# A fused attention and expert kernel on one core: rows for the experts gathered one block ahead instead of two, and the last attention pair's fills and value products in another order

## Chip, cores, metric

One Trainium2 chip, one of its cores. The metric is device time of one execution in microseconds (us), the median of several runs; smaller is better.

## What is computed

Attention with rotary embedding over 8 batches, 8 heads, 576 tokens, head width 64, and then a top-1 mixture of 8 experts on the 4608 resulting rows of 512 numbers:

```python
scores = q_rot @ k_rot.T / sqrt(D);  attn = softmax(scores);  x = attn @ v     # all heads side by side
logits = x @ w_gate + modality_bias[modality_id]                               # 4608 x 8
e_idx = argmax(logits);  gate_w = softmax(logits)[e_idx]
for e in range(E):
    mask = e_idx == e
    h = np.maximum(x[mask] @ w1[e], 0.0)                                       # 512 -> 1024
    out[mask] = gate_w[mask, None] * (h @ w2[e])                               # 1024 -> 512
```

Which token goes to which expert is known only on the chip.

## The kernel before

**Attention.** 32 pairs of heads, one about every 14.4 us. Each pair `n` has nine score tiles (`scores`, `rowmin`, `expo`), six *fills* (`fill`: the probabilities are transposed on TensorE into a ring of three two-bank PSUM tiles), two *evacuations* of each fill to SBUF (`evac`, one on ScalarE, one on VectorE), two value products (`AV`, half 0 = "AVA" for 256 columns, half 1 = "AVB" for 320), their copies (`avout`, "OTA" and "OTB"), the output transposes (`outp`) and the scaling (`ev`, "EVA" and "EVB"). The value products and the output transposes share the PSUM pool `psA` with two buffers, tag `pa`.

AVB reads the columns that fills F2, F3 and FB fill; AVA reads those of F0, F1 and FA.

**Routing.** After every fourth pair (a batch) the router ranks the rows of its batch by expert, and GpSimd scatters their numbers into a table in DRAM (`scatter`, five indirect DMAs a batch, "TAB" in the profile).

**Experts.** The table is read in blocks of 256 rows. 8 blocks are planned after five batches (they run first), 11 more after all eight: 19 blocks on this input. For each block `s`, eight indirect DMAs of GpSimd (`m_gather`, "XG<-X" at line 734) fetch 128 quarter rows each into `XG[s % 2]`; before the first of them a small GpSimd instruction makes the list of indices (`iy`, line 732). VectorE transposes both halves (`m_tr`, gathers 0 to 3 make the first half, 4 to 7 the second), ScalarE and VectorE split them into a high and a low part (`m_tre`); `m_split` does the same for the weights (`W1H` and `W2H` by ScalarE, `W1L` and `W2L` by VectorE). The first layer is four groups of 24 matmuls (`m_l1`, line 799; tiles psH, or ps for block 0), the second two groups of 24 (`m_l2`, line 816). The results are scaled by ScalarE into `y` (two buffers, line 819) and scattered to the output by GpSimd (line 820, "out_dram"). Each such scatter writes the same tensor as the one before it.

Engines keep the order of the program. In the attention part that order is sorted by due times written by hand (`KEYS` for a pair, with other values for single pairs in `AT`: `last` is the last pair, number 31); in the expert part it is the order of the loop in `chain`. With 31*14.438 us subtracted, an entry of `AT` is a due time in the frame of the last pair. Everything due after `end` = 12.0 is written behind the attention part; block 0's first layer (keys `l1`) is still in it.

In `chain`, block `s` begins with `m_rows(s + 2)`: all eight gathers of the block behind the next one. They wait for nothing but the list and for `m_tre(s)` having read the buffer. Block 1's eight gathers stand in the attention part (`rows[1]`, behind the first group of block 0's first layer) and those of block 2 at key 16.5, behind the first two scatters of batch 6 and ahead of its last three. Batch 7's five scatters come out of the list `late`, popped by `one()`: two at the end of block 1, three within the first layer of block 2.

Of the kernel before, what the change touches and what calls it, by code (L numbers as in the profile page):

```python
# [45 lines left out]
AT = dict(  # L46
    rk=(23.0, 28.55, 31.2, 36.9, 41.45, 43.0, 44.4, 45.7, 54.6, 56.9, 57.4, 58.85, 60.2, 70.35, 73.3),
    bias=15.6,
    sc=(73.4, 87.85, 102.3, 116.7, 116.75),
    sce=(73.4, 73.45, 87.85, 87.9, 102.3),  # L50
    pl=(58.9, 70.4, 73.35, 84.85, 87.75, 99.3, 102.2, 113.7, 116.6),
    plan=(-49.7, -35.2, 6.0, 9.0),
    ix=(-41.5, -3.9, 6.1, 9.1),
    sine=-48.9,
    rows=(((0, -27.5, None), (1, -13.05, None), (2, -12.4, None), (3, -2.9, (30, "av", 0)), (5, 0.45, (30, "av", 1)),
           (7, 4.75, (30, "out", 1))), ((0, 11.15, ("l1", 0)),), ((0, 16.5, None),)),
    w1=(-21.6, -21.5, -16.2, -16.1),
    w2=(-9.9, -9.8, -9.7, -9.6),
    hi=(-14.8, -14.7, -0.4, -0.3),
# [2 lines left out]
    te=(10.3, 10.4),  # L62
    hi2=(10.5, 10.98, 11.1, 11.2),
    lo2=(11.5, 11.55, 11.65, 11.75),
    last=dict(AVA=10.3, AVB=10.4, RE=10.2, RI=10.25, OTA=10.96, OTB=11.0, OUTB=11.2, OUTA=11.21, EVB=11.35, EVA=11.4, XO=11.9),
    l1=(11.1, 11.3, 11.4, 11.42),
    l1e=(11.3, 11.6, 11.7, 11.8),
    w1n=(11.85, 11.86, 11.87, 11.88),
# [2 lines left out]
    first=dict(S1=-5.9, S0=-5.86, MN1=-5.82, MN0=-5.74, EX1=-5.7, EX0=-5.66, S6=-5.58, S7=-5.54, MN6=-5.5,  # L71
        EX6=-5.42, MN7=-5.34, EX7=-5.3, S3=-5.26, S2=-5.22, MN3=-5.18, EX3=-5.14, F0=-5.1, MN2=-5.06,
        A_F0=-5.02, B_F0=-4.98, EX2=-4.94, F3=-4.9, S4=-4.86, A_F3=-4.82, B_F3=-4.78, MN4=-4.74, S5=-4.7,
        EX4=-4.66, MN5=-4.62, EX5=-4.58, S8=-4.54, MN8=-4.5, EX8=-4.46, LV=-2.9),
    second=dict(T1=-20.22, T2=-20.06, R=-19.9, HI=-19.82),
# [8 lines left out]
def tile_attention_moe(ctx: ExitStack, tc: tile.TileContext, qk, v, mod, wg, mb, w1, w2, rope, cf, ci, out):  # L84
# [23 lines left out]
    def cview(name):  # L108
        o, n = CF_OFF[name]
        return CF[:, o:o + n]  # L110
# [582 lines left out]
    def bank(kind):  # L693
        if kind in banks:
            return banks[kind].tile([P, 512], F32, name=f"ps{kind}", tag=f"ps{kind}")
        if not spare:
            ps = ring()[1]
            spare.extend(ps[:, i, :] for i in (1, 0))
        return spare.pop()
# [28 lines left out]
    def m_gather(s, t, g, after=None):  # L728
        d = ms[s]
        if "iy" not in d:  # L730
            d["iy"] = ixp.tile([P, 8], I32, name="iy", tag="iy")
            nc.gpsimd.tensor_scalar(d["iy"], d["xi"][:, :, 0], 4.0, cview("I4"), op0=ALU.mult, op1=ALU.add)
        rows = (N if slots[s][0] else NPL * S) * 4
        inst = nc.gpsimd.indirect_dma_start(out=XG[s % 2][:, t, g, :], out_offset=None,  # L734
                                            in_=X.rearrange("n (i f) -> (n i) f", f=P)[0:rows],
                                            in_offset=bass.IndirectOffsetOnAxis(ap=d["iy"][:, 2 * g + t:2 * g + t + 1], axis=0),
                                            bounds_check=rows - 1, oob_is_err=False)
        if after is not None:

            tc.add_manual_dep(inst.ins, (l1_[after[1]] if after[0] == "l1" else st[after[0]][after[1:]]).name,  # L740
                              mybir.DependencyInfo(mybir.DependencyClass.Sync, mybir.DependencyReason.DATA), reason="place")

    def m_rows(s):
        for t in range(2):
            for g in range(4):
                m_gather(s, t, g)

    def m_load1(s, g):
        d = ms[s]
        nc.sync.dma_start(out=ST1[:, :, g * 256:(g + 1) * 256],  # L750
                          in_=w1[bass.ds(d["e"], 1), :, g * 256:(g + 1) * 256].rearrange("o (c p) f -> p (o c) f", p=P), cond=d["c"])

    def m_load2(s, g):
        d = ms[s]
        nc.sync.dma_start(out=ST2[:, g * 2:g * 2 + 2, :],
                          in_=w2[bass.ds(d["e"], 1), g * 256:(g + 1) * 256, :].rearrange("o (c p) f -> p (o c) f", p=P), cond=d["c"])

    def m_hi(i, g):
        sl = slice(g * 256, (g + 1) * 256)
        if i == 0:  # L760
            acopy(W1[0][:, :, sl], ST1[:, :, sl])
        else:
            acopy(W2[0][:, g * 2:g * 2 + 2, :], ST2[:, g * 2:g * 2 + 2, :])

    def m_lo(i, g):
        sl = slice(g * 256, (g + 1) * 256)
        if i == 0:
            sub(W1[1][:, :, sl], ST1[:, :, sl], W1[0][:, :, sl].bitcast(F32))
        else:
            sl = slice(g * 2, g * 2 + 2)  # L770
            sub(W2[1][:, sl, :], ST2[:, sl, :], W2[0][:, sl, :].bitcast(F32))

    def m_split(i, g):
        m_hi(i, g)
        m_lo(i, g)
# [13 lines left out]
    def m_l1(s, g):  # L789
        d = ms[s]  # L790
        if g == 0:
            d["hh"], d["hl"] = HHL[s % 2]
        ps = bank("H").rearrange("p (c r) -> p c r", r=BLK)
        for i in range(2):
            f0 = (g * 2 + i) * P
            m = 0
            for c in range(4):
                for w, x in ((W1[0], XTH), (W1[0], XTL), (W1[1], XTH)):
                    l1_[s] = nc.tensor.matmul(ps[:, i, :], w[:, c, f0:f0 + P], x[:, c, :], start=(m == 0), stop=(m == 11)).ins  # L799
                    m += 1  # L800
        d["ps", g] = ps
# [24 lines left out]
    def J(k_, nm, n, f, *a):  # L826
        jobs.append((k_ + PER * n, len(jobs), f, a))
# [27 lines left out]
        load(2, half)  # L855
    z = NPAIR - 1

    OV = {0: AT["first"], 1: AT["second"], z: AT["last"]}
    for n in range(NPAIR):
        def K_(nm, f, *a):  # L860
            J(OV.get(n, {}).get(nm, K[nm]), nm, n, f, *a)

# [31 lines left out]
        if n % 4 == 3:  # L894
            K_("XO", xout, n // 4)
            g = route(n // 4)
            steps = [(next, g, None)] * (NRK - (n == z))
            scats = [(scatter, n // 4, j) for j in range(5)]
            if n == z:

                g = plan()
# [4 lines left out]
            if n == 4 * NPL - 1:  # L906
                g = plan0()
# [6 lines left out]
    def Z(k_, f, *a):  # L914
        J(k_, "moe", z, f, *a)

    A = AT
    fills = max(K[f] for f in K if f[0] in "SF")
    planned, tabled = (max(AT[c]) - (NPAIR - 4 * NPL) * PER for c in ("pl", "sc"))
    assert min(A["plan"]) > planned and min(A["ix"]) > tabled and min(A["w1"]) > max(K["T2"], K["LO"] - PER)  # L920
    assert min(A["w2"]) > max(K["T1"], K["LO"]) and min(A["te"]) > max(K[f"S{u}"] for u in range(9)) - PER
    assert min(A["hi2"]) > fills + 0.05 and min(A["lo2"]) > A["last"]["AVB"] + 0.05 and min(A["l1"]) > fills
    for s in range(len(A["plan"])):
        Z(A["plan"][s], m_plan, s)
    for s in range(4):
        Z(A["ix"][s], m_ix, s)
    for s in range(3):
        for i in range(8):
            k_, after = [x for x in A["rows"][s] if x[0] <= i][-1][1:]
            Z(k_ + 0.01 * i, m_gather, s, i // 4, i % 4, after)  # L930
# [27 lines left out]
    def prefetch(s):  # L958
        for i in range(3):
            m_plan(s + i)  # L960
        for g in range(4):
            m_load1(s, g)
        for i in range(3):
            m_ix(s + i)
        for i in range(2):
            m_rows(s + i)
        for g in range(4):
            m_load2(s, g)

    def chain(lo, hi, begun):  # L970
        if not begun:
            for g in range(4):
                m_split(0, g)
            for t in range(2):
                m_tr(lo, t)
                m_tre(lo, t)
        for s in range(lo, hi):
            nxt = s + 1 < hi
            if nxt:
                if s + 2 < hi and (not begun or s > 0):  # L980
                    m_rows(s + 2)
                if s + 3 < hi and (not begun or s > 0):
                    if s + 3 not in ms:
                        m_plan(s + 3)
                    m_ix(s + 3)
                for g in range(4):
                    if not begun or s > 0:
                        m_load1(s + 1, g)
            if not begun or s > lo:
                for g in range(4):  # L990
                    m_split(1, g)
                    m_l1(s, g)
                    m_l1e(s, g)
                    one()
            if nxt:
                for t in range(2):
                    m_tr(s + 1, t)
                for t in range(2):
                    m_tre(s + 1, t)
                    one()  # L1000
                for g in range(4):
                    m_load2(s + 1, g)
            if not begun or s > lo:
                m_l2(s, 0)
            if nxt:
                m_split(0, 0)
                one()
                m_split(0, 1)
                one()
            m_l2(s, 1)  # L1010
            if nxt:
                m_split(0, 2)
                one()
                m_split(0, 3)
                one()
# [108 lines left out]
```

## Time and profile before

| | |
|---|---|
| three runs | 937.27, 939.65, 940.5 us; median 939.65 |
| the profiled execution | 946.46 us, of which the span 944.7 us from first to last instruction |
| mean granted TensorE clock | 0.995 |
| TensorE matmuls (PE) | 903.4 us busy, 96% of the span, 9248 instructions |
| VectorE (DVE) | 670.6 us, 71% |
| ScalarE (ACT) | 629.9 us, 67% |
| GpSimd (POOL) | 669.0 us, 71%, 498 instructions |
| gathers, line 734 | 152, 1235 ns mean |
| scatters to the output, line 820 | 38, 1128 ns mean |

The attention part ends at about 500 us, the rest is the expert blocks. PE is busy almost everywhere, so the time is the sum of PE's work and of the gaps in it; the gaps lie between 486 and 561 us, in the passage from one part to the other. In rows of the profile "idle before <-X" names what ended an engine's idle time; "issue" is time in which it waited for nothing that the profile shows.

### The profile page before, as it was taken

What the parts mean: (1) busy time and instruction counts of PE and PEld (TensorE: products, weight loads), DVE (VectorE), ACT (ScalarE), POOL (GpSimd) and SP (SyncE); (2) the same over time, 40 slices, a digit from 0 to 9 for tenths busy, and PEclk for the clock granted to TensorE, in tenths of its full rate; (3) what the DMA queues carried; (4) which work ended last, traced back from release to release, by engine and by line L of the source; (5) the groups of instructions that cost most, each with busy time, mean ns of one, the idle gap of its engine ahead of it and who ended that gap; (6) DMA issues with size and microseconds to landing.
All of it is one profiled execution on the core that took longest, in us unless ns stands there. A gap on an engine that the chain in (4) does not pass through costs nothing. (4 is left out here: it accounts for less than half of the span.)

```text
span 944.7 us, 24944 instructions
## 1 busy us (share of the span) xinstructions
PE 903.4 (96%) x9248; PEld 740.9 (78%) x9248; DVE 670.6 (71%) x1165; ACT 629.9 (67%) x1292; POOL 669.0 (71%) x498
## 2 busy tenths in 40 slices
PE   2999999999999999999989999999999999999996
PEld 2777777777777777777667878888888899999995
DVE  6677778787787877877784768676666766666661
ACT  2778778787787877878881555565665656666561
POOL 3988879888888898999723768766676656666400
PEclk9999999999999999999999999999999999999998
DMA  8865758768586686855922621117711611251100
GB/s 261 237 185 166 236 159 213 188 167 229 162 222 165 183 213 175 232 163 154 244 98 73 186 72 35 46 57 229 230 51 51 229 40 45 90 190 45 37 24 16
DMA packets 79292, 136.90 MB, mean 145 GB/s; under 512 B 28699, under 2 KB 50603, under 8 KB 78140
## 3 DMA queue, kind: packets, MB, share of 16 engines
q1 hardware_dynamic: 68460, 114.06, 42.8%
q0 software_dynamic: 9440, 19.46, 6.3%
q10 hardware_dynamic: 1264, 1.72, 0.6%
q8 instruction: 75, 1.23, 0.6%
q14 instruction: 53, 0.43, 0.2%
HBM read 140.59 MB, written 19.77 MB: 170 GB/s over the span
## 5 line engine op out<-in xcount | busy, mean ns | idle before, releaser
L328 ACT ACTIVATE P<-ps,mn 128x576 f32<-128x576 f32 x288 | 210.4, 737 | 92.4 <-DVE mn L321 91.9
L321 DVE TENSOR_REDUCE mn<-ps 128x1 f32<-128x576 f32 x288 | 204.1, 745 | 93.5 <-PE ps L312 55.6
L734 POOL DMA_INDIRECT XG<-X,iy x152 | 187.7, 1235 | 70.9 <-issue 53.5
L799 PE MATMUL psH<-HL,W1H 128*128 128x256 f32 x1152 | 205.5, 281 | 1.0 <-issue 0.7
L312 PE MATMUL ps<-SW 64*128 64x288 f32 x960 | 166.5, 314 | 16.0 <-DMA SW<-HL 16.0
L799 PEld LDWEIGHTS psH<-HL,W1H 128*128 128x128 f32 x1152 | 177.9, 188 | 4.1 <-issue 2.5
L312 PE MATMUL ps<-HL 64*128 64x288 f32 x960 | 166.4, 312 | 1.0 <-ACT P L328 0.8
L799 PE MATMUL psH<-HL,W1L 128*128 128x256 f32 x576 | 161.7, 281 | 1.4 <-issue 0.8
L312 PEld LDWEIGHTS ps<-SW 64*128 64x128 f32 x960 | 134.2, 189 | 27.4 <-DMA SW<-HL 15.5
L312 PEld LDWEIGHTS ps<-HL 64*128 64x128 f32 x960 | 136.4, 189 | 22.7 <-issue 13.6
L269 DVE TENSOR_TENSOR W1L<-ST,W1H 128x1024 fp32r<-128x1024 f32 x76 | 90.1, 1222 | 80.6 <-ACT W1H L272 77.5
L390 PE MATMUL pa<-PH,V 128*64 128x320 f32 (+1 forms) x1024 | 138.3, 412 | 2.7 <-ACT oT L272 1.4
L820 POOL DMA_INDIRECT out_dram<-y,ix x38 | 42.9, 1128 | 129.7 <-ACT y L819 97.4
L816 PE MATMUL psY<-W2H,SW 128*128 128x512 f32 x304 | 121.2, 399 | 0.0
L816 PE MATMUL psY<-W2L,SW 128*128 128x512 f32 x304 | 119.9, 394 | 0.0
L334 PE MATMUL ps<-idf,P 64*128 64x64 f32 x2624 | 105.3, 229 | 8.5 <-ACT P L328 2.8
L334 PEld LDWEIGHTS ps<-idf,P 64*128 64x128 f32 x2624 | 92.2, 140 | 23.8 <-ACT PH L272 9.5
L799 PEld LDWEIGHTS psH<-HL,W1L 128*128 128x128 f32 x576 | 108.4, 188 | 1.8 <-issue 1.0
L289 POOL TENSOR_TENSOR HL<-ST,HL 128x1216 fp32r<-128x1216 f32 x31 | 86.1, 2777 | 31.8 <-ACT HL L272 31.7
L390 PEld LDWEIGHTS pa<-PH,V 128*64 128x64 f32 x1024 | 68.1, 136 | 51.1 <-issue 10.1
L366 DVE COPY PH<-ps 128x512 f32<-128x512 f32 (+1 forms) x160 | 96.0, 633 | 8.9 <-PE ps L334 7.6
L269 DVE TENSOR_TENSOR W2L<-ST,W2H 128x1024 fp32r<-128x1024 f32 x76 | 92.6, 1219 | 5.2 <-ACT W2H L272 4.3
(173 smaller groups left out, 1589.9 us busy)
## 6 DMA issues: line engine op xcount, KB each, us to landing
ST<-in_moe_w_dram SPq DMA_DIRECT2D x152, 512.0 KB
ST<-in_qk_dram SPq DMA_DIRECT2D x62, 608.0 KB
SW<-HL SPq DMA_DIRECT2D x124, 232.0 KB
V<-in_v_dram SPq DMA_DIRECT2D x32, 256.0 KB
X<-X SPq DMA_DIRECT2D x8, 1024.0 KB
XG<-X,iy POOLq DMA_INDIRECT x152
V<-in_v_dram SPq DMA_DIRECT2D x64, 16.0 KB
X<-XT SPq DMA_DIRECT2D x16, 64.0 KB
```

The lines of the kernel that those rows point to most:

```text
L269: nc.vector.tensor_tensor(o, a, b, op=ALU.subtract)
L289: e.tensor_tensor(d["HL"][:, 1, c], a, d["HL"][:, 0, c].bitcast(F32), op=ALU.subtract)
L312: free(nc.tensor.matmul(ps[:, g, 0:288], t[:, wq, q0:q0 + P], t[:, wk, k0:k0 + 288], start=(m == 0), stop=(m == len(L) - 1)), seen)
L321: lastmin[d["ring", u]] = nc.vector.tensor_reduce(mn, d["S", u][:, :, 0:288], op=ALU.min, axis=AX.XY).ins
L328: nc.scalar.activation(p.rearrange("p (a b) -> p a b", a=2), ps[:, :, 0:288], AF.Exp, bias=d.pop(("m", u)), scale=-1.0, accum_out=d["sum"] ...
L334: free(nc.tensor.transpose(ps[0][:, g, c:c + 64], src[r, k0:k0 + P], idf[r, r]), ps[1])
L366: mine.append((nc.vector.tensor_copy if g else acopy)(o, i).ins)
L390: i = nc.tensor.matmul(pa[hh * 64:hh * 64 + 64, 0:c1 - c0], d["V"][:, hh, kt, :], r, start=(kt == 0), stop=(kt == 4))
L734: inst = nc.gpsimd.indirect_dma_start(out=XG[s % 2][:, t, g, :], out_offset=None, in_=X.rearrange("n (i f) -> (n i) f", f=P)[0:rows], in_o ...
L799: l1_[s] = nc.tensor.matmul(ps[:, i, :], w[:, c, f0:f0 + P], x[:, c, :], start=(m == 0), stop=(m == 11)).ins
L816: nc.tensor.matmul(ps, hx[:, c, t * P:(t + 1) * P], w[:, c, :], start=(m == 0), stop=(m == 23))
L820: nc.gpsimd.indirect_dma_start(out=out, out_offset=bass.IndirectOffsetOnAxis(ap=d["ix"][:, t, 0:1], axis=0), in_=y, in_offset=None, bounds ...
```

## The change

Three edits.

1. **Gathers.** `m_rows` is gone. In `chain`, block `s` now gathers for block `s + 1`, two gathers ahead of each group of the first layer; from the second pair on, each waits for the last first-layer matmul written so far, that is for the group before. The gathers of block 1 in the attention part are spread the same way (one pair behind each of the four groups of block 0), and those of block 2 leave their place ahead of batch 6's last three scatters for the loop.
2. **Last pair.** Its fills go in the order F3, F0, F2, FB, FA, F1 (before: F3, F0, FA, F2, FB, F1), with their evacuations; AVB stands ahead of AVA, and their copies likewise.
3. **Last pair but one.** Its EVA moves from due time 25.51 to 24.55 (10.11 in the last pair's frame, just ahead of both value products; before it was due at 11.07, behind them).

```diff
-    rows=((...), ((0, 11.15, ("l1", 0)),), ((0, 16.5, None),)),
+    rows=((...), ((0, 11.15, ("l1", 0)), (2, 11.33, ("l1", 0)), (4, 11.365, ("l1", 0)), (6, 11.43, ("l1", 0)))),
...
-    last=dict(AVA=10.3, AVB=10.4, RE=10.2, RI=10.25, OTA=10.96, OTB=11.0, OUTB=11.2, OUTA=11.21, EVB=11.35, EVA=11.4, XO=11.9),
+    last=dict(F2=7.0, A_F2=7.75, B_F2=7.75, FB=7.5, A_FB=8.3, B_FB=8.3, FA=8.35, A_FA=8.8, B_FA=8.8, AVB=10.3, AVA=10.4, RE=10.2,
+              RI=10.25, OTB=10.96, OTA=11.0, OUTB=11.2, OUTA=11.21, EVB=11.35, EVA=11.4, XO=11.9),
+    last2=dict(EVA=24.55),
...
-    def m_rows(s):
-        for t in range(2):
-            for g in range(4):
-                m_gather(s, t, g)
...
-    OV = {0: AT["first"], 1: AT["second"], z: AT["last"]}
+    OV = {0: AT["first"], 1: AT["second"], z - 1: AT["last2"], z: AT["last"]}
...
-    for s in range(3):
+    for s in range(2):
         for i in range(8):
             k_, after = [x for x in A["rows"][s] if x[0] <= i][-1][1:]
             Z(k_ + 0.01 * i, m_gather, s, i // 4, i % 4, after)
...
-                if s + 2 < hi and (not begun or s > 0):
-                    m_rows(s + 2)
...
                 for g in range(4):
                     m_split(1, g)
+                    if nxt:
+                        for i in (2 * g, 2 * g + 1):
+                            m_gather(s + 1, i // 4, i % 4, ("l1", s) if g else None)
                     m_l1(s, g)
                     m_l1e(s, g)
                     one()
```

More of the change, by code (lines that the diff above doesn't have):

```diff
@@ L55 @@
     rows=(((0, -27.5, None), (1, -13.05, None), (2, -12.4, None), (3, -2.9, (30, "av", 0)), (5, 0.45, (30, "av", 1)),
-           (7, 4.75, (30, "out", 1))), ((0, 11.15, ("l1", 0)),), ((0, 16.5, None),)),
+           (7, 4.75, (30, "out", 1))), ((0, 11.15, ("l1", 0)), (2, 11.33, ("l1", 0)), (4, 11.365, ("l1", 0)), (6, 11.43, ("l1", 0)))),
     w1=(-21.6, -21.5, -16.2, -16.1),
@@ L921, in tile_attention_moe @@
     assert min(A["w2"]) > max(K["T1"], K["LO"]) and min(A["te"]) > max(K[f"S{u}"] for u in range(9)) - PER
-    assert min(A["hi2"]) > fills + 0.05 and min(A["lo2"]) > A["last"]["AVB"] + 0.05 and min(A["l1"]) > fills
+    assert min(A["hi2"]) > fills + 0.05 and min(A["lo2"]) > A["last"]["AVA"] + 0.05 and min(A["l1"]) > fills
     for s in range(len(A["plan"])):
@@ L964, in prefetch @@
             m_ix(s + i)
-        for i in range(2):
-            m_rows(s + i)
+        for i in range(8):
+            m_gather(s, i // 4, i % 4)
         for g in range(4):
```

## The prediction, made before the changed kernel ran

> **What bounds the kernel now.** PE is busy for 96% of the span, so first its list of waits (us in total, times, longest):
>
> ```profile
> PE ps L799 <- issue: 2.1, 4, 0.9
> PE pa L390 <- ACT oT L272: 1.4, 1, 1.4
> PE pa L390 <- ACT re L406: 1.3, 1, 1.3
> ```
>
> Then the windows of first layers (us, PE busy, matmuls; granted clock PEclk): blocks 0, 2 and 13, and the second layer of block 2:
>
> ```profile
> 497.46:514.68 17.22, 13.67 (x96) 12.54 (x96) 0.92 0.31 99
> 550.10:565.31 15.21, 13.45 (x96) 11.99 (x96) 1.00 0.15 49
> 801.47:812.73 11.26, 11.26 (x96) 11.22 (x95) 1.00 0.12 41
> 565.31:576.50 11.19, 11.19 (x48) 8.83 (x48) 1.00 0.16 38
> ```
>
> A block is 11.26 + 11.19 = 22.45 us of PE with no gap. Block 0's first layer is 17.22, 5.96 over: 2.1 of "issue" (the list), 1.7 of a half clock (below), the rest mostly the last pair's output transposes, which stand inside it. Block 2's is 15.21, 3.95 over. The late block loses nothing. What the change can gain lies in these two layers and in front of the first; what it can lose lies wherever the gathers stop being early. So the third view is GpSimd's timeline from block 0's second layer on (start, duration; some rows left out):
>
> ```profile
> 521.79 1.02 POOL L820 DMA_INDIRECT out_dram<-y,ix  x1 [9.85 <-ACT y L819]
> 526.27 1.79 POOL L537 DMA_INDIRECT TAB<-VAL,oi  x1 [0.31 <-issue]
> 529.34 1.79 POOL L734 DMA_INDIRECT XG<-X,iy  x1 [0.27 <-POOL iy L732]
> ...
> 540.60 1.00 POOL L734 DMA_INDIRECT XG<-X,iy  x1 [0.30 <-issue]
> 541.90 1.01 POOL L537 DMA_INDIRECT TAB<-VAL,oi  x1 [0.30 <-issue]
> ...
> 545.74 0.98 POOL L820 DMA_INDIRECT out_dram<-y,ix  x1 [0.30 <-issue]
> ...
> 559.24 1.98 POOL L820 DMA_INDIRECT out_dram<-y,ix  x1 [0.31 <-issue]
> 565.80 1.68 POOL L820 DMA_INDIRECT out_dram<-y,ix  x1 [4.57 <-issue]
> ...
> 571.34 1.10 POOL L734 DMA_INDIRECT XG<-X,iy  x1 [0.27 <-POOL iy L732]
> ...
> 589.11 0.92 POOL L537 DMA_INDIRECT TAB<-VAL,oi  x1 [0.31 <-issue]
> ```
>
> GpSimd is late here: block 0's second scatter to the output goes at 545.74, 24 us behind the first at 521.79, where PE needs 5.6 (half of 11.19) for what it scatters. That costs little because gathers run one block further ahead than they must. Only block 2's gathers, the last ending at 541.60, were late, and that wait ends last in block 2:
>
> ```profile
> 546.73 0.71 DVE L779 STREAM_TRANSPOSE XG<-XG 128x512 f32<-128x512 f32 x1 [3.80 <-DMA XG<-X,iy]
> 548.44 0.66 ACT L819 ACTIVATE y<-psY,ix 128x512 f32<-128x512 f32 x1
> 550.08 1.23 DVE L269 TENSOR_TENSOR W1L<-ST,W1H 128x1024 fp32r<-128x1024 f32 x1
> 551.37 0.39 PE L799 MATMUL psH<-HL,W1L 128*128 128x256 f32 x1 [0.76 <-issue]
> ```
>
> From the second transpose to the first matmul with the low weights: 551.37 - 546.73 = **4.64 us** (ScalarE has the second split, `y` and the first weights in that order). One more delay is needed, from the last gather to that transpose, where the transpose waited for it:
>
> ```profile
> 611.58 0.99 POOL L734 DMA_INDIRECT XG<-X,iy  x1 [0.30 <-issue]
> 614.23 0.71 DVE L779 STREAM_TRANSPOSE XG<-XG 128x512 f32<-128x512 f32 x1 [1.88 <-DMA XG<-X,iy]
> ```
>
> 614.23 - 612.57 = **1.66 us**. So the first layer of a block can go 6.3 us after its last gather ends; its third matmul is where it stops, 0.24 (two matmuls of 11.26/96) after its start.
>
> **The change, part by part.** *Last pair.* Rows of the passage:
>
> ```profile
> 490.81 1.95 PE L390 MATMUL pa<-PH,V 128*64 128x256 f32 x16 [1.28 <-ACT re L406]
> 494.62 2.38 PE L390 MATMUL pa<-PH,V 128*64 128x320 f32 x16 [1.43 <-ACT oT L272]
> 488.53 1.03 DVE L366 COPY PH<-ps 128x512 f32<-128x512 f32 x2
> 490.03 0.68 DVE L366 COPY PH<-ps 128x512 f32<-128x512 f32 x1
> 492.55 2.11 DVE L269 TENSOR_TENSOR HL<-XG,HL 128x512 fp32r<-128x512 f32 x2 [0.53 <-ACT HL L272]
> 496.84 0.41 DVE L437 TENSOR_TENSOR X<-pa,ri 128x256 f32<-128x256 f32 x1
> ```
>
> AVA waits for the copy of F1 (to 490.71), AVB for a PSUM buffer that AVA's copy frees, because the other is held until EVA of pair 30 at 496.84. With AVB first, F1 (and FA) are no longer in its way: it starts behind FB's copies at about 489.9, takes 497.46 - 494.62 = 2.84, and AVA follows without a wait, its buffer freed by the moved EVA, in some 2.35 (the 1.95 and four matmuls more, an estimate): PE is free at 495.1. The moved EVA puts about 0.6 on VectorE ahead of the transposes, so the split of block 0's rows ends at 494.66 + 0.65 = 495.3. The first layer starts there and not at 497.46: **-2.1** (bounds -2.7, both waits whole; -1.2, if the copies behind it on ScalarE come no sooner).
>
> *Block 0.* Four pairs behind four groups in place of eight in a row; the last pair ends 2.6 us (two of 1.0 + 0.3) behind the layer and lands 1.7 later, and by ScalarE's order the split of those rows stands behind `y` of block 0's first half, 5.6 us behind the layer. Cost 0. Whether the 3.8 of stall and half clock stay I can't derive (no row names a releaser): 0, bounds -3.8 and 0.
>
> *Block 2's gathers.* Batch 6's last three scatters and the output scatter at 545.74 now go first. From 526.27: 2.1, three scatters at 1.3 to 1.5, the output scatter 1.3, the list 0.9, then eight gathers in the 12.3 that they take now (529.34 to 541.60): the last ends near 547.1, the transpose is at 548.8, PE goes at 553.4 where it could at 550.34: a wait of 3.1, against 3.95 lost now. **-0.9** (bounds: nothing blocked on GpSimd, 1.3 each, no loss, -3.9; the present stall on top of the wait, +2).
>
> *Block 3's gathers*, now behind a chain that starts with block 2's. `y` of block 1 comes 548.44 - 546.73, 1.7 us after the late transpose by ScalarE's order, so its first output scatter goes at 551.2. The next must land behind it: 3.6 to 6.6 start to start (559.24 to 565.80 is 6.56); I take 3.8. Two scatters of batch 7 and the list: to 560. Then eight gathers and batch 7's other three scatters, interleaved, which take 571.34 to 590.03 = 18.7 now and 11 x 1.3 = 14.3 with no blocking; I take 16.5: 576.5. Plus 6.3: PE can go at 582.8. It would be ready at 550.10 + 3.1 + 22.45 + 0.24 = 575.9. Now this block waits for nothing. **+6.9** (bounds 3.7 and 9.2). All these times shift by -2.1 together, the chain hangs on `y` of block 0.
>
> *The clock behind that wait.* The stall in block 0 was followed by a half clock:
>
> ```profile
> 512.00:513.00 1.00, 0.70 (x4) 0.39 (x2) 0.00 (x0) 0.00 (x0) 0.00 (x0) 0.50 0.24 66
> 515.00:516.00 1.00, 1.00 (x5) 0.77 (x5) 0.45 (x1) 0.52 (x1) 0.00 (x0) 0.79 0.00 0
> ```
>
> Half clock through 512 to 515 and 0.79 in the next us: 3 x 0.5 + 0.21 = 1.7 us lost. The same behind the wait of block 3: **+1.7** (bounds 0 and 3.4, both blocks). The Trainium skill (TensorE: Matmul & The Clock Gate, Part 1) has the array's clock halved after an idle window of about 3.4 us and restored after as long a busy one; by it the wait of 6.9 costs the 1.7 and the one of 3.1 nothing, as taken, and this rule speaks against the change.
>
> *Later blocks.* A late block, when GpSimd has caught up:
>
> ```profile
> 803.75 2.05 POOL L732 TENSOR_SCALAR iy<-xi,CF 128x8 int32<-128x8 int32 x1
> 803.39 2.36 DVE L269 TENSOR_TENSOR W1L<-ST,W1H 128x1024 fp32r<-128x1024 f32 x2 [3.23 <-ACT W1H L272]
> 806.08 1.76 POOL L734 DMA_INDIRECT XG<-X,iy  x1 [0.27 <-POOL iy L732]
> 816.73 1.35 POOL L734 DMA_INDIRECT XG<-X,iy  x1 [0.30 <-issue]
> ```
>
> The block started at 801.47, so gathers run from 4.6 to 16.6 after its start (later than the groups that they would wait for, so the new waits bind nothing). Those rows are now for the next block: 16.6 + 1.66 + 4.64 = 22.9 against the 22.45 + 0.24 = 22.7 when PE wants them: 0.2 short. As a late block gives the next one's gathers that much more time, it is paid every second block, 8 times; and the last gather takes 1.0 and not 1.35 if VectorE isn't subtracting beside it. **+0.5** (bounds 0 and 4).
>
> Sum: -2.1 - 0.9 + 6.9 + 1.7 + 0.5 = **+6.1** on the profiled execution's 946.46. That execution lies 6.8 above the median of 939.65, and the stalls without a releaser (3.8 and part of 3.95) may be what it has over the others; I carry the difference, less 0.5 for block 0's open end, to the median: **945.3**.
>
> **Rivals.**
>
> A, *GpSimd keeps up, and the order wins* (faster). If VectorE's subtractions block GpSimd less, every gather and scatter takes 1.0 + 0.3: block 2 loses nothing (-3.9), block 3 waits 3.7 without a clock drop, and the "issue" stalls, which stand beside runs of eight gathers, go with them (-3.8): -2.1 - 3.9 + 3.7 - 3.8 = -6.1, 933.5; without the last, 937.3. For it: rows of 1.00 exist wherever VectorE is idle. Against: in first layers it is not. It decides if block 3's last gather ends before about 572. [...]
>
> B, *a wash*: the last pair gives its 2.1, block 2 1 to 2, block 3 costs only 3.7: 939 to 941.
>
> C, *gathers never early again*: the 0.2 is 0.7, or landings beside weight loads take longer; the transposes come late in every block, 8 x 0.7 = 5.6 on the sum: 950. For it: 22.9 against 22.7. Against: block 4 ran so without a gap, its last gather ending at 612.57, 13.6 after its start.
>
> **How the numbers follow.** Forecast (block 3 waits over 4 us) 0.5; A 0.16; B 0.2; C 0.14. About 0.3% (2.8 us) is what a measurement of this kernel can tell from no change. A is faster (0.15 and a bit within); B same; C slower; of the forecast's 0.5 some 0.48 is slower. Faster 0.15, same 0.21, slower 0.64. The range, 937.5 to 950, leaves out half of A and the end of C; the forecast alone holds 942.5 to 948.5.
>
> **What would show it.** The first layer of block 0 starting at 495 or so; AVB ahead of AVA without idle time; block 2 waiting about 3 us for its rows; a gap of about 7 us in front of or in block 3's first layer, with a VectorE transpose "<-DMA XG" and a half clock behind it; later blocks at 22.45 to 22.6. Wrong if block 3 starts without a wait, which means that GpSimd's chain is shorter than I add up, or if block 0's stall goes.

## The result, and the profile after

The kernel after takes **952.2 us** (median; 950.41 to 955.09) where the one before takes 939.43 (937.27 to 940.5): ratio **1.015**, 95% interval 1.0129 to 1.0171, slower by 12.8 us. The forecast was 945.3, slower by 5.9, with a range up to 950. The sign was right and so was the place where most is lost; the size was not.

The profiled execution of after took 952.66 us, within the range of its others. Its windows, in the columns shown before (us, PE, weight loads, VectorE, ScalarE, GpSimd, granted clock, DMA share, GB/s): first layer of block 0; second layer of block 1 and first of block 2; second of block 2 and first of block 3; then blocks 1 to 3 together, and all that comes behind them:

```profile
494.30:507.71 13.41, 13.25 (x118) 12.65 (x117) 8.44 (x13) 4.58 (x7) 6.39 (x6) 1.00 0.35 111
531.48:544.69 13.21, 11.38 (x51) 8.84 (x49) 4.57 (x9) 4.46 (x7) 6.73 (x7) 1.00 0.59 200
544.69:557.08 12.39, 11.63 (x96) 11.43 (x97) 11.24 (x13) 8.83 (x11) 8.58 (x7) 1.00 0.16 49
557.08:574.88 17.80, 11.36 (x50) 8.84 (x49) 5.54 (x15) 4.26 (x6) 10.81 (x11) 0.92 0.24 27
574.88:590.63 15.75, 14.53 (x97) 14.01 (x97) 14.03 (x29) 8.94 (x11) 11.02 (x10) 0.77 0.16 55
518.90:601.84 82.94, 72.03 (x440) 63.80 (x439) 54.03 (x90) 40.22 (x50) 50.51 (x42) 0.94 0.35 90
601.84:941.97 340.13, 338.94 (x2160) 305.14 (x2159) 225.85 (x234) 194.69 (x236) 186.77 (x156) 1.00 0.28 93
```

An undisturbed second layer is 11.19 and a first one 11.26. Block 2 waits (13.21 - 11.19) + (12.39 - 11.26) = 3.15 us for its rows. Block 3 loses (17.80 - 11.19) + (15.75 - 11.26) = **11.1**: the wait, and a clock of 0.77 behind it. The stall that block 0's layer had in the profile of before (17.22 us) isn't there.

What stands ahead of block 3 on GpSimd (timeline; start, duration, and idle time before it with its releaser):

```profile
543.97 1.30 POOL L817 DMA_INDIRECT out_dram<-y,ix  x1 [4.96 <-ACT y L816]
547.80 1.42 POOL L817 DMA_INDIRECT out_dram<-y,ix  x1 [2.54 <-ACT W1H L274]
549.53 1.96 POOL L539 DMA_INDIRECT TAB<-VAL,oi  x1 [0.31 <-DVE W1L L271]
551.79 1.42 POOL L539 DMA_INDIRECT TAB<-VAL,oi  x1 [0.30 <-issue]
...
554.87 1.08 POOL L736 DMA_INDIRECT XG<-X,iy  x1 [0.27 <-POOL iy L734]
...
566.36 0.93 POOL L539 DMA_INDIRECT TAB<-VAL,oi  x1 [0.30 <-issue]
...
568.91 1.00 POOL L736 DMA_INDIRECT XG<-X,iy  x1 [0.30 <-issue]
```

Block 1's two output scatters, two scatters of batch 7 into the table, then eight gathers with three more of those scatters among them: the last gather ends at 569.91. VectorE takes over, and PE:

```profile
571.53 0.71 DVE L776 STREAM_TRANSPOSE XG<-XG 128x512 f32<-128x512 f32 x1 [5.24 <-DMA XG<-X,iy]
574.88 1.10 PE L796 MATMUL psH<-HL,W1H 128*128 128x256 f32 x2 [6.44 <-ACT W1H L274]
577.20 0.58 PE L796 MATMUL psH<-HL,W1L 128*128 128x256 f32 x1 [1.22 <-DVE W1L L271]
```

PE names the weights as releaser, but these stand on ScalarE and VectorE behind the split of rows that the transpose at 571.53 let go: the wait is one for rows. In PE's whole list of waits it comes right behind the wait for the kernel's first loads, which before has too (16.0 us in all):

```profile
PE ps L314 <- DMA SW<-HL: 15.8, 4, 13.5
PE psH L796 <- ACT W1H L274: 8.3, 2, 6.4
PE psH L796 <- DVE W1L L271: 3.7, 5, 1.2
```

The two waits for values of the last pair (1.4 and 1.3 before) and all "issue" waits in first layers are gone from that list.

### The profile page after: what moved, and what is told of

The parts are those of the page before. It is cut to its first block, busy times and chain, and to the rows that moved or that the text cites. A ratio compares the mean times of both kernels' runs of the same rounds, so it can differ in the third digit from the quotient of the medians.

```text
span 950.7 us, 24968 instructions
## 1 busy us (share of the span) xinstructions
PE 905.7 (95%) x9248; PEld 743.9 (78%) x9248; DVE 673.1 (71%) x1165; ACT 628.4 (66%) x1292; POOL 659.9 (69%) x498
## 5 line engine op out<-in xcount | busy, mean ns | idle before, releaser
L736 POOL DMA_INDIRECT XG<-X,iy x152 | 173.1, 1139 | 69.6 <-issue 50.7
L796 PE MATMUL psH<-HL,W1H 128*128 128x256 f32 x1152 | 208.0, 283 | 8.3 <-ACT W1H L274 8.3
L314 PEld LDWEIGHTS ps<-HL 64*128 64x128 f32 x960 | 137.6, 190 | 22.3 <-issue 12.8
L817 POOL DMA_INDIRECT out_dram<-y,ix x38 | 49.1, 1293 | 144.2 <-ACT y L816 107.9
L274 ACT ACTIVATE HL<-XG 128x512 fp32r<-128x512 f32 x38 | 42.8, 1132 | 104.9 <-DVE XG L776 104.9
```

The lines of the kernel that those rows point to most:

```text
L314: free(nc.tensor.matmul(ps[:, g, 0:288], t[:, wq, q0:q0 + P], t[:, wk, k0:k0 + 288], start=(m == 0), stop=(m == len(L) - 1)), seen)
L817: nc.gpsimd.indirect_dma_start(out=out, out_offset=bass.IndirectOffsetOnAxis(ap=d["ix"][:, t, 0:1], axis=0), in_=y, in_offset=None, bounds ...
```

## The experiments

They ran in three groups. The kernels of a group share a chip and its runs of the kernel before, whose median was 947.37 us in the first group, 937.82 in the second and 937.36 in the third. So ratios are compared within a group. A ratio is taken over the single runs and can differ by some 0.002 from the quotient of two medians.

| group | kernel | ratio to before | 95% interval |
|---|---|---|---|
| 1 | before_again | 0.9996 | 0.9963 to 1.0028 |
| 1 | last_only | 0.9945 | 0.9909 to 0.9981 |
| 1 | gather_only | 1.0100 | 1.0061 to 1.0139 |
| 1 | scats_later | 0.9990 | 0.9959 to 1.0020 |
| 2 | after_again | 1.0147 | 1.0126 to 1.0169 |
| 2 | eight_in_row | 1.0133 | 1.0115 to 1.0152 |
| 2 | last_pairs | 0.9977 | 0.9963 to 0.9991 |
| 2 | two_then_one | 1.0022 | 1.0006 to 1.0037 |
| 3 | before_third | 1.0002 | 0.9991 to 1.0012 |
| 3 | last_only_2 | 0.9972 | 0.9959 to 0.9985 |
| 3 | last_pairs_2 | 0.9966 | 0.9952 to 0.9980 |
| 3 | scats_later_2 | 1.0070 | 1.0053 to 1.0087 |

**Was the stall in every execution of before?** The forecast was summed on a profiled execution of 946.46 us with a stall in block 0 and another in block 2. The kernel before, unchanged, was profiled on two more chips. In the first group (948.6 us median, this execution 946.87):

> The kernel before, unchanged, for a second profiled execution. Theory 1 (the profiled execution of before, 946.46, held stalls that its other executions lack): near 939.5, and block 0's first layer is near 13.4 instead of 17.21, with no 'issue' wait of PE worth more than 0.5 us, and block 2's first layer is shorter than 15.2. Theory 2 (every execution has these stalls and the execution above was slow elsewhere): block 0's first layer again 17 us and block 2's 15, whatever the time.

```profile
499.12:516.36 17.24, 14.94 (x118) 13.92 (x117) 5.84 (x10) 3.52 (x5) 8.52 (x8) 0.91 0.31 99
551.60:563.95 12.35, 11.60 (x97) 11.39 (x97) 11.22 (x13) 8.90 (x11) 9.78 (x8) 1.00 0.16 43
```

Block 0's stall is back, 17.24 us, in an execution of the same length; block 2's is not (12.35 for 15.21). As this execution is near 946 again, it tells the theories apart only for block 2: that stall isn't in every one. The third group does it for block 0 (937.3 us median, this execution 936.99):

> The kernel before once more, for a profile on a chip where it takes 938 and not 947. Theory (the stalls of block 0's and block 2's first layers belong to the executions near 946, and the 937.8 of the chip where after is 1.5% slower lacks them): if this profiled execution is at 936 to 940, block 0's first layer is 13.4 and block 2's under 13, without a wait of PE for 'issue' in first layers; if it is at 945 to 948, both are there, as in the two profiled so far. Rival (the stalls are in all executions of before, and 938 is gained elsewhere): 17.2 in an execution at 938.

```profile
495.43:508.61 13.18, 13.03 (x118) 12.62 (x117) 5.84 (x10) 3.53 (x5) 7.49 (x7) 1.00 0.37 118
543.67:555.83 12.16, 11.65 (x98) 11.45 (x96) 10.97 (x13) 8.48 (x11) 9.53 (x8) 1.00 0.13 39
519.82:589.63 69.81, 68.58 (x440) 61.55 (x438) 52.38 (x89) 40.19 (x50) 52.49 (x42) 1.00 0.36 103
589.63:926.29 336.66, 336.66 (x2160) 304.06 (x2159) 224.63 (x236) 196.00 (x236) 195.43 (x157) 1.00 0.29 95
```

No stall: 13.18 for 17.22 in block 0 and 12.16 for 15.21 in block 2. With block 0 starting at 495.43 for 497.46 that is 2.0 + 4.0 + 3.0 = 9.1 of the 9.5 us between the two executions. Theory held: an execution of before at 937 has neither stall, and after was timed against executions at 937 to 940.

**The last pair alone.** Before, with `last=` and `last2=` of after:

```diff
-    last=dict(AVA=10.3, AVB=10.4, RE=10.2, ...),
+    last=dict(F2=7.0, ..., AVB=10.3, AVA=10.4, RE=10.2, ...),
+    last2=dict(EVA=24.55),
```

> Only the last pair's order (fills, values of half B first, the normalisation of pair 30 earlier), with before's gathers. The trace of after has the first layer starting at 494.3 against 497.46: 3.2 us sooner. If the gain of this part is whole and nothing behind it takes it back: 939.4 - 3.2 = 936.2. Rival (block 2's first layer waits for rows that hang on GpSimd and not on PE, so that an earlier start is only waited for there): 939, no change. If block 0's stall of 3.8 us is in every execution of before and the last pair's order removes it: 932.5.

> The same kernel as last_only (0.9945 on a chip with before at 947.4). On a chip with before at 937.8: theory 1 (the pairs matter only where block 0 stalls) 0.9977, that of last_pairs; rival (the four pairs cost or gain by themselves) another ratio than last_pairs by 0.002 or more. The first layer starts 3 us sooner than before's on the same chip; if the total gains less, it is lost again in block 0 or 2.

Group 3: 0.9972, 934.8 us, **2.6 us** less than before. In group 1 it is 0.9945 (943.3 us), with block 0's first layer at 17.13: the part gains, and doesn't remove that stall.

**The gathers alone.** After, with the three tables of the last pair as in before (the reverse of the diff above):

> Only the gathers for the next block, with before's last pair. After is 952.2; if its last pair gives 3.2 us, this one is at 955.4. Rival (the chain on GpSimd sets block 3, so that a last pair later by 3.2 us is partly hidden in block 3's wait): 952.5 to 953.5. If the last pair's order cost something: under 952.

1.0100, 958.84 us. In this group the two parts sum to 0.9945 + 0.0100 = 1.0045 (by the medians to 1.0078), less than the 1.0147 of the whole change in the second group. One reason is in the traces: here before has block 0's stall and this kernel, on the same chip, has not:

```profile
498.38:511.52 13.14, 12.98 (x118) 12.59 (x117) 5.84 (x10) 3.53 (x5) 6.40 (x6) 1.00 0.36 113
```

That is 4.1 us, or 0.0043, of a difference of 0.0102; the rest stays open. The runs of this group scatter more than those of the others (before: 943 to 956 us), and after itself did not run here. Its execution also has a stall that no other trace has: block 4's second layer (614.54 to 631.53) takes 16.99, 5.8 over 11.19, with PE waiting there for ScalarE:

```profile
PE psY L811 <- ACT SW L802: 2.4, 1, 2.4
```

**After again, on a chip without the stall.**

> The kernel after, unchanged, to be compared with before and with its own parts on one chip. Theory 1 (the parts add up: last pair 0.9945, gathers 1.010): 1.0045 of before. Theory 2 (the gain of block 0's stall and of the last pair is lost again in the waits behind it, as the first comparison had it): 1.015 of before, and later blocks again 3 us or more over 22.45 each in sum.

The number is that of theory 2: 1.0147, 951.7 us against 937.8. So the loss is not of one chip only. Its reason, a gain that is lost again in the waits behind it, this run alone does not show.

**One run of eight gathers, or four pairs.** After, with block 1's gathers as before had them:

```diff
-  ((0, 11.15, ("l1", 0)), (2, 11.33, ("l1", 0)), (4, 11.365, ("l1", 0)), (6, 11.43, ("l1", 0)))
+  ((0, 11.15, ("l1", 0)),)
```

and last_pairs: last_only with the four pairs in place of that one run.

> After, with block 1's eight gathers in one run behind block 0's first group, as before has them; all else as after. Block 0's first layer was 17.2 us in three executions with the run of eight and 13.1 to 13.4 in three with four pairs. Theory 1 (the run of eight makes the stall): block 0's first layer is 17 us again with half clock in it, y of block 0 and all that hangs on it 3.8 us later, 3.8 us over after_again. Rival (what makes the stall is something else in before's order of instructions, its runs of gathers two blocks ahead among it): 13.4, and the time of after_again.

> Before's gathers two blocks ahead, the last pair's order of after, and block 1's gathers in four pairs behind block 0's four groups. Theory 1 (the run of eight makes block 0's stall): first layer of block 0 13.4 instead of 17.1, 3.8 us less than last_only: 0.9945 - 0.0040 = 0.9905 of before. Rival (something else in before's order makes it): 17.1 and 0.9945.

> The same kernel as last_pairs, for which the ratio was 0.9977 on a chip with before at 937.8. Where before is at 937.8: 0.9977 again. Where before is at 947 (block 0's stall in it): if the run of eight makes that stall where it appears, 0.9945 - 0.0040 = 0.9905; if not, 0.9945.

In groups 2 and 3 block 0's first layer is 13.3 to 13.5 with either form, and the time is the same within the intervals: 1.0133 beside 1.0147, and 0.9966 beside 0.9972. Theory 1 falls for these chips. Before doesn't stall there either: its trace shows it for the third group, and for the second only its time of 937.8 speaks for it. For the chip where it does stall, nothing is settled: neither kernel ran there.

**Batch 7's scatters behind block 3's gathers.** The edit is made to after. Six steps of the second plan now go ahead of the scatters as well:

```diff
-  late = steps + scats + [(each, next) + ((g, None),) * 4] * 7
+  rest = [(each, next) + ((g, None),) * 4] * 7
+  late = steps + rest[:6] + scats + rest[6:]
```

> After, with batch 7's five scatters into the table behind block 3's gathers (six steps of the second plan go ahead of them). Theory 1 (GpSimd's chain with these five scatters sets block 3's wait): five scatters at 1.3 to 1.8 us leave the chain, the last gather for block 3 ends near 562 instead of 569.9, block 3 waits 1 to 3 us instead of 9.0 and there is no half clock: 952.2 - 8.5 = 943.5 (942 to 946). Rival (the chain hangs on the output scatters behind the rows' y, and the scatters into the table only fill its idle time): 952.2 - 2 = 950 or no change.

> The same kernel as scats_later, which was 0.999 of before on a chip with before at 947.4, where the gathers alone were 1.010. Against after at 1.0147 on a chip with before at 937.8: theory 1 (batch 7's five scatters are what block 3 waits behind) 8 us less, 1.006; rival (other work on GpSimd sets block 3) 1.012 to 1.015.

Group 3: 1.0070 against after's 1.0147 (group 2, with before at the same time), 7.2 us less (8.5 by the medians). Block 2's second layer, block 3's first, and the second of block 3, then the last gather for block 3:

```profile
554.96:566.17 11.21, 11.21 (x50) 8.88 (x49) 7.41 (x17) 4.36 (x6) 8.01 (x7) 1.00 0.10 25
566.17:578.52 12.35, 11.59 (x97) 11.39 (x97) 11.09 (x11) 8.78 (x11) 9.86 (x10) 1.00 0.17 56
578.52:589.84 11.32, 11.32 (x51) 8.84 (x49) 4.43 (x7) 4.33 (x6) 5.77 (x6) 1.00 0.13 36
```

```profile
560.12 1.00 POOL L736 DMA_INDIRECT XG<-X,iy  x1 [0.30 <-issue]
```

Block 3 loses 1.1 where it lost 11.1, and the clock stays at 1.00. The last gather for it ends at 561.12, 8.8 us earlier than after's; block 0 started 1.95 earlier (492.35), so the edit itself gave 6.8, which is five scatters of 1.4. What block 3 waits for is GpSimd's queue, and these scatters are most of the wait. In group 1 the same edit gave 0.999, beside a before with block 0's stall. The execution profiled there (953.26 us) lost nothing in block 3 either, but 6.9 with a half clock in block 2, and that loss is not explained.

**Early blocks or late ones.** last_only, with gathers two blocks ahead for blocks 2 to 5 and after's pairs from block 5 on:

```diff
-  if s + 2 < hi and (not begun or s > 0):
+  if s + 2 < 6 and (not begun or s > 0):
       m_rows(s + 2)
...
       m_split(1, g)
+      if nxt and s >= 5:
+          for i in (2 * g, 2 * g + 1):
+              m_gather(s + 1, i // 4, i % 4, ("l1", s) if g else None)
       m_l1(s, g)
```

> As the kernel with the last pair's order alone, up to block 5; from block 5 on the gathers are for the next block, two ahead of each group, as in after. By then GpSimd has caught up (its scatters into the table are done). Theory 1 (one block ahead is too short in every other block: what after's trace has as 3.1 us from block 4 on and the two others with these gathers as 8 to 10): 4 to 8 us over last_only, 0.9945 + 0.004 to 0.008 = 0.9985 to 1.003 of before. Rival (these losses are GpSimd's lag from the first blocks, handed on): the time of last_only, 0.9945, and 22.45 us for each block.

1.0022, as theory 1 has it: 0.0045 over last_pairs, **4.2 us** (2.9 by the medians), for one block ahead from block 6 on. What is left to after, 0.0125 or **11.7 us**, belongs to the gathers of blocks 2 to 5. From block 4 to the end two_then_one takes 340.90 and last_pairs 336.57, 4.3 more, and VectorE's transposes of the rows say why (count, us busy, mean ns, and what they waited for; two_then_one first, then last_pairs, over the same stretch):

```profile
L781 DVE STREAM_TRANSPOSE XG<-XG 128x512 f32<-128x512 f32 x28 | 19.9, 709 | 65.2 <-DMA XG<-X,iy 65.2
```

```profile
L781 DVE STREAM_TRANSPOSE XG<-XG 128x512 f32<-128x512 f32 x28 | 18.2, 686 | 0.6 <-DMA XG<-X,iy 0.6
```

The windows from block 4's start to the end of the last block, in the same order:

```profile
587.84:928.74 340.90, 338.07 (x2155) 303.97 (x2154) 227.45 (x236) 194.44 (x237) 187.26 (x157) 1.00 0.28 94
```

```profile
587.61:924.18 336.57, 336.57 (x2161) 303.98 (x2159) 223.21 (x234) 195.80 (x236) 195.43 (x156) 1.00 0.29 95
```

With rows two blocks ahead the transposes wait 0.6 us for gathers; with one ahead 65 us, and PE feels 4 of them. One of the two blocks whose successors lose most, which started at 861.66:

```profile
867.75 2.03 POOL L736 DMA_INDIRECT XG<-X,iy  x1 [1.74 <-issue]
870.09 1.35 POOL L736 DMA_INDIRECT XG<-X,iy  x1 [0.30 <-issue]
...
878.25 1.00 POOL L736 DMA_INDIRECT XG<-X,iy  x1 [0.30 <-issue]
880.83 0.71 DVE L781 STREAM_TRANSPOSE XG<-XG 128x512 f32<-128x512 f32 x1 [4.54 <-DMA XG<-X,iy]
```

Its last gather ends 17.6 us after the block's start, and the next block's first layer takes 12.39, 1.1 over.

**The version to keep** is last_pairs: 0.9977 and 0.9966, 936.9 and 934.9 us. It is faster than before by 0.2 to 0.3%, with both intervals just below 1, and faster than after by 1.7%; last_only can't be told from it.

## Why the prediction was right or wrong

By stages, the profiled execution of after (952.66) against that of before_third (936.99): 494.30 for 495.43 at block 0's start, 24.60 for 24.39 in block 0, 82.94 for 69.81 in blocks 1 to 3, 340.13 for 336.66 behind them: -1.1 + 0.2 + 13.1 + 3.5 = 15.7.

- **Last pair, -2.1: right.** Alone it gives -2.6 (group 3; -3.8 to -1.4 by the interval). In after AVB (320 columns) goes ahead of AVA, and PE has no idle time from there to block 0 at 494.30:

```profile
489.30 2.38 PE L392 MATMUL pa<-PH,V 128*64 128x320 f32 x16
492.05 1.90 PE L392 MATMUL pa<-PH,V 128*64 128x256 f32 x16
```

  The starts of block 0 in single executions can't size this term: with this order and outside group 1 they lie between 492.35 and 495.16.
- **Block 0, 0: right** where before takes 937 to 940, since neither kernel has the stall there (13.18 in before_third). It was a choice and not a result: the prediction says that it could not derive it. Against the profiled execution of before it was wrong by 3.8: after's layer is 13.41.
- **Block 2, -0.9: the first step that failed.** The wait of 3.1 was right to a tenth (3.15), but in the wrong way: the chain began with `y` of block 0, which came earlier than taken, and the last gather ended at 539.01 and not 545; PE, with no stall in block 0, was ready earlier too. What failed is "against 3.95 lost now". Those 3.95 were of one execution; the two others of before that were profiled lose 1.1 and 0.9 there. The credit was 3.0 too large. The text said that the stalls may be what the execution had over the others, and then carried the difference to the median nearly whole, although one stall stood in it as a gain.
- **Block 3, +6.9, and +1.7 for the clock: right in kind, too small.** A gap in front of it, a transpose "<-DMA XG" and a half clock are all there. They cost 11.1 for 8.6 here (8.7 of wait and 2.4 of clock, worked out below), and 6.1 and 8.4 in after_again and eight_in_row. Blocks 2 and 3 together: 14.3, 12.1 and 13.7 where the terms were 11.7. One piece of the difference: from the second transpose to the first low-weight matmul it took 577.20 - 571.53 = 5.7 for the 4.64 taken; VectorE has short steps of the second plan between its split of the rows and the weights' subtraction there, but that they are the reason was not tried. The 1.62 from gather to transpose (569.91 to 571.53) was as taken.
- **The clock.** Windows of two us around the wait:

```profile
568.00:570.00 2.00, 0.44 (x2) 0.00 (x0) 0.00 (x0) 0.00 (x0) 1.61 (x2) 1.00 0.41 31
570.00:572.00 2.00, 0.00 (x0) 0.00 (x0) 0.47 (x1) 0.00 (x0) 0.00 (x0) 0.96 0.11 35
572.00:574.00 2.00, 0.00 (x0) 0.00 (x0) 1.90 (x6) 1.67 (x3) 0.00 (x0) 0.50 0.01 4
580.00:582.00 2.00, 2.00 (x11) 2.00 (x11) 1.93 (x6) 0.00 (x0) 1.72 (x2) 0.50 0.35 131
582.00:584.00 2.00, 2.00 (x19) 2.00 (x18) 2.00 (x3) 1.54 (x2) 1.69 (x2) 0.98 0.11 33
```

  PE stopped at 568.44 (574.88 - 6.44); by these shares the clock was halved at 571.8, 3.4 us later, and was back at 582.1, 4.9 after the third matmul. Block 3's layer is 15.75; its third matmul came 2.32 behind its first for 0.24, which is 2.1 of wait. That leaves 13.67 for 11.26: 2.4 for the half clock and not 1.7. The Trainium skill (TensorE: Matmul & The Clock Gate, Part 1) has an idle window of about 3.4 us for the fall; this trace agrees. But that a wait of 3.1 costs no clock, as taken, does not always hold: block 2's was free in after (1.00 above), and in after_again a wait of 3.4 there cost another 2.7 of half clock (last part).
- **Later blocks, +0.5: the second step that failed, too small though about at its upper bound.** It is 3.5 here, 2.8 and 4.1 in after_again and eight_in_row, 4.2 by the ratios of two_then_one. It is not 0.2 in every second block either: in after, blocks 7, 8, 11 and 17 lose 0.4 to 1.3 each and the others next to nothing. The second transpose comes 18.3 us after the block's start on the mean of blocks 4 to 17, as taken (16.6 + 1.66), but it varies from 17.8 to 19.2, and PE pays for the late ones. A sum with one typical block could not show that. Rival C had the mechanism with 5.6; the truth lies between.
- **The sum.** The +6.1 met +6.2 (952.66 - 946.46) by errors that cancel: block 0's stall went (-3.8), block 3 cost 2.5 more, the later blocks 2.6 (340.13 for 337.01), the last pair gave 1.1 more. Against an unstalled before the same terms give -2.1 + (3.1 - 0.9) + 8.6 + 0.5 = +9.2, where the medians have +12.8. So 3.3 of the miss of 6.9 is the baseline, and the remaining 3.6 the sizes of the waits and of the later blocks. That +6.1 came out as +6.2 was luck.
- **Rival A** fell, though its sign came: the last gather ended at 569.91, before the 572 that it names. Eight gathers and three scatters took 15.0 us, near its pace; but PE, with no stall in block 0, had stopped for them at 568.44, and the queue ahead of the gathers made block 3 late.

## What to carry to other kernels

Before a stall of the profiled execution is booked as something that a change can win, look whether the execution is as long as the timed ones: if it is 0.7% over them, its odd waits, those without a releaser above all, may well be the difference (here they were 7.1 of 9.5 us), and the sum has to be made without them on both sides. A queue that serves two purposes (here gathers for the next layer, and scatters that nobody waits for yet) needs its prefetch distance counted in queue entries: with its own eight gathers and the outputs in front, one block ahead was short by some 4 us in thirteen blocks, and with five scatters in front as well by 10 us in one. Moving the work that can wait helps, 7.2 us here by one small edit, but gathers two blocks ahead were worth more: 11.7 in blocks 2 to 5 and 4.2 behind them.

## What the runs showed of the hardware

The same kernel took 947.4, 937.8 and 937.4 us on three chips. Of the first difference 4 us have a place: a stall in block 0's first layer, with no releaser, seen there in before (17.24) and last_only (17.13) and not, on the same chip, in gather_only (13.14) or scats_later (13.44). Another 3.7 lie ahead of that layer (before_again starts it at 499.12, before_third at 495.43). The profiled execution of before at 946.46 has the stall too; on which chip it ran is not on record. What makes it stays open. The two kernels that have it gather two blocks ahead and fetch block 1's rows in one run of eight, the two without do neither; and gather_only has a stall of its own, in block 4. The two later chips showed it in no profiled kernel, with gathers two blocks ahead or one.

A wait of 2.2 us, with a second one of 0.5 behind it, was enough for a half clock. In after_again, in front of block 2's first layer (timeline of PE, then windows):

```profile
543.05 0.40 PE L813 MATMUL psY<-W2L,SW 128*128 128x512 f32 x1
545.62 0.80 PE L796 MATMUL psH<-HL,W1H 128*128 128x256 f32 x2 [2.18 <-ACT W1H L274]
546.88 0.58 PE L796 MATMUL psH<-HL,W1L 128*128 128x256 f32 x1 [0.46 <-DVE W1L L271]
```

```profile
542.10:545.50 3.40, 1.35 (x6) 0.75 (x4) 3.00 (x5) 2.50 (x5) 0.60 (x1) 1.00 0.00 0
544.00:546.00 2.00, 0.38 (x1) 0.38 (x2) 1.65 (x4) 2.00 (x4) 1.10 (x1) 0.87 0.00 0
550.00:552.00 2.00, 2.00 (x12) 2.00 (x11) 1.57 (x2) 0.01 (x1) 1.70 (x2) 0.50 0.35 131
552.00:554.00 2.00, 2.00 (x17) 2.00 (x17) 1.13 (x2) 1.53 (x2) 1.61 (x3) 0.92 0.01 1
```

By these shares the clock fell at 545.5, 2.0 us after PE stopped (545.62 - 2.18 = 543.44) and just before it resumed, and was back at 552.3, behind five us of dense matmuls. That layer took 14.94, 3.68 over 11.26: 1.0 of wait (1.26 from the first matmul to the third, for 0.24) and 2.7 for the clock. In after the same place had waits of 1.83 and 0.76 by the timeline and kept its clock. In eight_in_row, with a wait of 2.31 there, the clock fell only about 548.2, when PE had been at work again. The stretch of 3.4 us up to that fall, and in after the stretch that ends eight times 3.41 us ahead of its fall at 571.8:

```profile
544.80:548.20 3.40, 1.66 (x11) 1.45 (x12) 3.21 (x6) 3.40 (x5) 1.30 (x1) 1.00 0.20 77
```

```profile
541.10:544.50 3.40, 1.76 (x8) 1.09 (x6) 2.99 (x5) 2.37 (x3) 0.53 (x1) 1.00 0.00 0
```

PE was busy for 1.35 and 1.66 us in the two stretches that ended in a half clock, and for 1.76 in the one that didn't: the border would lie at half of the stretch. The Trainium skill (TensorE: Matmul & The Clock Gate, Part 1) calls the window free-running, 3413 ns long, and speaks of an idle one; by these rows a half idle one is enough. But the border is not sharp. Two more stretches of 3.41 us, cut by the falls of their own traces, lie on the wrong side of it: in scats_later PE was busy for 1.90 us (756.23 to 759.64) and the clock was halved behind it, in last_pairs_2 for 1.55 (923.94 to 927.36, its last matmuls) and the clock stayed.

The ends of matmuls are modelled in these traces, so PE's busy time is rough. "About half" is an estimate from these five cases and not a rule.
